# Reordering the first tile of a fused retention and gated-FFN kernel: wider zero products, keys and queries loaded ahead of values, one copy split over two engines

## The chip, the cores and the metric

The kernel runs on one core of one Trainium2 chip. A core has five instruction streams that run beside each other and meet only at semaphores: PE (matrix products; its weight loads are a track of their own, PEld), DVE and ACT (both copy and compute, and both read the accumulator banks that PE writes), POOL (GpSimd, which here also issues most of the transfers), and SP (which issues transfers only). The time of a run is the time on the device in microseconds, here from the one core that is used; a kernel's figure is the median over its runs. The profile is of one such run, and carries its own time.

## The reference, cut to what matters

Four batches of eight heads, 768 positions, 64 wide. First a recurrent retention with one decay per head, then a gated feed-forward layer over its output:

```python
gamma = 1.0 - 2.0 ** (-5.0 - np.arange(H))
for t in range(S):
    state = gamma * state + einsum('bhd,bhe->bhde', k[:, :, t], v[:, :, t])
    y[:, :, t] = scale * einsum('bhd,bhde->bhe', q[:, :, t], state)
x = y.transpose(0, 2, 1, 3).reshape(B * S, H * D)
gate = 1.0 / (1.0 + np.exp(-(x @ w_gate)))     # 512 -> 1536
out = (gate * (x @ w_val)) @ w_out              # 1536 -> 512
```

## The kernel before, in words

The 768 positions are cut in six tiles of 128 positions (`NT = 6`). A tile has the same 128 positions of all four batches, so the feed-forward layer sees 512 tokens per tile. Within a tile the retention is worked in two groups `i` of two batches `j` each; the texts below number the four as chunk 0 to 3, and write (i, j) for them. For a chunk, keys and queries are turned on PE (four products with the identity for each), copied out of the accumulator banks to `kqT`, multiplied to scores (eight half-height products), multiplied by a decay mask on DVE to bfloat16 (`st`, two instructions of 512 columns), and multiplied with the values to the outputs `y` (eight products). The scaled outputs of the four chunks fill the columns of `xT`, which the layer's products (`up_part`, L349: four products of 512 columns per gate or value column block) read. `down` (L376) is the layer's second product. PE's products write into eight accumulator banks that are handed out in turn (`pf`).

The program is in an order written out by hand: each engine runs its instructions in the order of the code. The first tile has code of its own, which the change is all about:

- L104 and L105 load keys and queries of chunk 0 in float32 through the queues of SP and ACT. L109 loads the other chunks, cast to bfloat16, through POOL, which takes them one after the other; L112 to L114 put the first six pieces of the gate and value weights behind them on the same queue. Piece 0 of the gate weights is what the very first `up_part` reads.
- L132 and L133 make `zero`, a constant of zeros. `keep_on` (L400) multiplies zeros with zeros into a bank that nobody reads. It is called eleven times before the layer's first product, with 3 to 40 products in a call, 104 in all.
- L137 to L151 make the constants on DVE and ACT, among them `decay`, and cast chunk 0. `later_constants` (L153), `later_exps` (L164), `last_exps` (L168, the table `taby` that tile 1 onward uses in `y_out`) and `last_constants` (L161) make the rest, in the midst of the first tile.
- `first_transpose` (L302), `first_scores` (L309) and `first_y` (L315) are the three steps of a chunk; their last argument is the engine that copies the result. L408 to L448 string them together. `first_scaled` (L326, POOL) and `first_state` make the state that the second tile needs; the sigmoid's table is loaded on ACT at L437.
- L449 begins the layer for tile 0.

Of the kernel before, what the change touches and what calls it, by code (L numbers as in the profile page):

```python
# [9 lines left out]
BF16 = mybir.dt.bfloat16  # L10
AX = mybir.ActivationFunctionType
ALU = mybir.AluOpType
# [3 lines left out]
def kernel(  # L16
# [12 lines left out]
    nc = tc.nc  # L29
# [4 lines left out]
    NT = S // C  # L34
    NP = H // 2
# [3 lines left out]
    scale = 1.0 / math.sqrt(D)  # L39
# [3 lines left out]
    const = ctx.enter_context(tc.tile_pool(name="const", bufs=1))  # L43
# [37 lines left out]
    def load_gate_val(s):  # L81
        load_w(wg, moe_w_gate, s)
        load_w(wv, moe_w_val, s)
# [7 lines left out]
    def first(dst, x, b, n, eng):  # L91
        eng.dma_start(out=dst, in_=x[b:b + n, :, 0:C, :].rearrange("b h s d -> s (b h) d"))  # L92
# [8 lines left out]
    def entry(t, j):  # L101
        return t[:, j * H:(j + 1) * H, :]
# [3 lines left out]
    nc.scalar.preload_act_table(AX.Exp)  # L106
    ahead = const.tile([128, C], F32, name="ahead")
    nc.gpsimd.iota(ahead, pattern=[[-1, C]], base=0, channel_multiplier=1, allow_small_or_imprecise_dtypes=True)
    for x, b in ((k, 1), (q, 1), (k, 2), (q, 2), (v, 0), (k, 3), (q, 3), (v, 1), (v, 2), (v, 3)):  # L109
        tiles = kn if x is k else qn if x is q else vs  # L110
        first(entry(tiles[b // 2], b % 2), x, b, 1, nc.gpsimd)
    load_gate_val(0)  # L112
# [6 lines left out]
    nlg = const.tile([128, 2, NP], F32, name="nlg")  # L119
    lgz = const.tile([128, 2, NP], F32, name="lgz")  # L120
    lsc = const.tile([128, 1], F32, name="lsc")
    tok = const.tile([128, NT], F32, name="tok")
    col = const.tile([128, C], F32, name="col")
    ident = const.tile([128, 128], BF16, name="ident")
    causal = const.tile([128, 128], F32, name="causal")
    decay = const.tile([128, 2, NP, C], F32, name="decay")
    maskk = const.tile([128, 2, NP, C], F32, name="maskk")
    tabs = const.tile([128, H, NT], F32, name="tabs")
    tabsk = const.tile([128, NT, 2, H], F32, name="tabsk")
    taby = const.tile([128, NP, C], F32, name="taby")  # L130
    tabz = const.tile([128, NT, 2, NP], F32, name="tabz")
    zero = const.tile([128, 128], BF16, name="zero")  # L132
    nc.vector.memset(zero, 0.0)  # L133
    nc.vector.memset(lsc, math.log(scale))
    for h in range(H):
# [11 lines left out]
    nc.vector.tensor_scalar(col, ahead, ahead[:, 0:1], -1.0, op0=ALU.subtract, op1=ALU.mult)  # L147
    for t in range(NT):
        nc.vector.tensor_scalar(tok[:, t:t + 1], ahead[:, 0:1], float(t * C), None, op0=ALU.add)
    nc.vector.tensor_copy(entry(kn[0], 0), kf)  # L150
    nc.scalar.copy(entry(qn[0], 0), qf)  # L151

    def later_constants():  # L153
        nc.vector.tensor_tensor(tabs.rearrange("s (p e) t -> s p e t", e=2),
                                tok.unsqueeze(1).unsqueeze(1).to_broadcast([128, NP, 2, NT]),
                                nlg.rearrange("s e p -> s p e").unsqueeze(3).to_broadcast([128, NP, 2, NT]), op=ALU.mult)

        for t in range(1, NT):
            nc.vector.tensor_scalar(tabz[:, t], lgz, float(t * C), None, op0=ALU.mult)

    def last_constants():  # L161
        nc.vector.tensor_scalar(causal, ahead, 0.0, None, op0=ALU.is_le)

    def later_exps():  # L164
        nc.scalar.activation(tabs, tabs, AX.Exp)
        nc.scalar.activation(tabz[:, 1:], tabz[:, 1:], AX.Exp)

    def last_exps():  # L168
        for p in range(NP):
            nc.scalar.activation(taby[:, p], col, AX.Exp, bias=lsc, scale=lgz[:, 0, p:p + 1])  # L170

    def later_tables():
        src = tabs.rearrange("s (p e) t -> s e t p", e=2)
# [12 lines left out]
    def bank(shape, dt=F32):  # L186
        return pf.tile(shape, dt, tag="ff", name="ff")

    def half(e):
        return slice(e * D, (e + 1) * D)  # L190

    def heads(t, j, p):
        return t[:, j * H + 2 * p:j * H + 2 * p + 2, :].rearrange("s h d -> s (h d)")

    def new_kqT(i):
        kqT[i] = at.tile([128, 2, 2, NP, C], BF16, tag="kqT", name="kqT", bufs=2)
# [19 lines left out]
    def scores(i, j):  # L216
        t = kqT[i]
        sc[i, j] = (bank([128, NP, C]), bank([128, NP, C]))
        for p in range(NP):
            for e in range(2):  # L220
                nc.tensor.matmul(sc[i, j][e][:, p, :], t[half(e), 0, j, p, :], t[half(e), 1, j, p, :],  # L221
                                 start=True, stop=True)
# [79 lines left out]
    def first_transpose(i, j, which, eng):  # L302
        x = (kn[i], qn[i])[which]
        tp = bank([128, NP, C], BF16)
        for p in range(NP):
            nc.tensor.transpose(tp[:, p, :], heads(x, j, p), ident)
        eng(kqT[i][:, which, j], tp)

    def first_scores(i, j):  # L309
        scores(i, j)  # L310
        for e, st in enumerate((stA, stB)):
            st[i, j] = at.tile([128, NP, C], BF16, tag=f"st{e}", name=f"st{e}", bufs=4)
            nc.vector.tensor_tensor(st[i, j], sc[i, j][e], decay[:, e], op=ALU.mult)  # L313

    def first_y(i, j, eng):  # L315
        if 0 not in xT:
            xT[0] = at.tile([128, NP, 512], BF16, tag="xT", name="xT")
        o = bank([128, NP, C])
        for p in range(NP):
            for e, st in enumerate((stA, stB)):  # L320
                nc.tensor.matmul(o[half(e), p, :], vs[i][:, j * H + 2 * p + e, :], st[i, j][:, p, :],  # L321
                                 start=(p == 0), stop=True, skip_group_check=True)
        c = (2 * i + j) * C
        eng(xT[0][:, :, c:c + C], o)
# [75 lines left out]
    def keep_on(n):  # L400
        u = bank([128, 512])
        for _ in range(n):
            nc.tensor.matmul(u[:, :128], zero, zero, start=True, stop=True)  # L403

    act, dve = nc.scalar.copy, nc.vector.tensor_copy
    new_kqT(0)  # L408
    new_kqT(1)
    keep_on(40)  # L410
    first_transpose(0, 0, 0, dve)
    first_transpose(0, 0, 1, act)
    later_constants()
    keep_on(3)
    first_transpose(0, 1, 0, act)
    first_scores(0, 0)
    first_transpose(0, 1, 1, act)
    keep_on(7)
    first_scores(0, 1)
    first_transpose(1, 0, 0, act)  # L420
    keep_on(3)
    first_transpose(1, 0, 1, act)
    keep_on(6)
    first_y(0, 0, act)
    later_exps()
    first_scores(1, 0)
    keep_on(4)
    first_transpose(1, 1, 0, act)
    last_exps()
    keep_on(5)  # L430
    first_transpose(1, 1, 1, dve)
    keep_on(6)
    first_y(0, 1, act)
    first_scores(1, 1)
    keep_on(6)
    first_y(1, 0, act)
    nc.scalar.preload_act_table(AX.Sigmoid)  # L437
    keep_on(12)
    first_y(1, 1, dve)
    last_constants()  # L440
    first_scaled(0, 0, kf)
    first_scaled(0, 1, entry(kn[0], 1))
# [2 lines left out]
    first_scaled(1, 1, entry(kn[1], 1))  # L445
    load_gate_val(4)
    load_gate_val(5)
    keep_on(12)  # L448
    for n1 in (0, 2, 4):  # L449
        gates = [up_part(0, wg, (n1 + i,)) for i in range(2)]  # L450
        for i in range(2):
# [111 lines left out]
```

## Time and profile before

| | |
|---|---|
| median of 4 runs | 229.94 us (229.79 to 230.27) |
| the profiled execution | 229.79 us |
| its span, first to last instruction | 228.0 us |
| PE busy | 220.1 us (97% of the span) |
| DVE, ACT, POOL busy | 110.0, 71.8, 104.0 us |
| first product of the layer (L349) starts | 16.92 us into the span |

The profile gives, per engine, what it did and what ended its idle times. Its parts used here are: the page's sums; the chain of waits, which starts at the last instruction and goes back, at each step, to whatever released it; the timeline, which lists the instructions of an engine in order of time with start and duration in us; and the transfers, with the time from the start of the issuing instruction to the landing of the data. A product on PE is recorded from its start to its end, some 0.2 us later, while the next ones have already started; so the distance between starts is what a product costs in a row of them. All times in the text are counted from the span's start.

### The profile page before, as it was taken

Reading aid. Unit: us, or ns where it says so; the run is one execution under the profiler, and the core shown is the slowest. Engines: PE = TensorE matmul, PEld = TensorE weight load, DVE = VectorE, ACT = ScalarE, POOL = GpSimd, SP = SyncE. Lnnn points to the kernel's source line nnn. Section 1 sums busy time; section 2 is a strip of 40 time slices with the busy share of each in tenths; the row PEclk is TensorE's granted clock in tenths of the full one; section 3 lists DMA queues with packets and bytes.
Section 4 is the critical chain, followed back from the end, with each engine's and each line's share of the span. In section 5 each row is a group of like instructions: output and inputs, shape, how many; then the busy total and the mean of one; then the engine's idle time right before and its main releaser. Section 6 shows DMA issues by size and latency. Waiting matters only on the chain.

```text
span 228.0 us, 4478 instructions
## 1 busy us (share of the span) xinstructions
PE 220.1 (97%) x1834; PEld 122.1 (54%) x1856; DVE 110.0 (48%) x198; ACT 71.8 (31%) x120; POOL 104.0 (46%) x125
## 2 busy tenths in 40 slices
PE   7789999999999999999999999999999999999994
PEld 7664444558888655445445445445444444444444
DVE  6663563064763776834905634914444812343301
ACT  4784233336323111332321433311433311433221
POOL 8999769999949969149930063000000000000000
PEclk9999999999999999999999999999999999999999
DMA  9999999999999999999992899012620012100022
GB/s 127 152 171 197 196 197 160 165 205 196 112 141 166 127 178 193 177 128 107 98 104 92 105 164 103 3 46 92 106 36 0 3 46 92 46 4 0 0 92 92
DMA packets 103636, 25.19 MB, mean 110 GB/s; under 512 B 92608, under 2 KB 100672, under 8 KB 103616
## 3 DMA queue, kind: packets, MB, share of 16 engines
q0 software_dynamic: 80896, 13.90, 82.8%
q1 hardware_dynamic: 21536, 10.69, 23.1%
q10 hardware_dynamic: 1184, 0.33, 0.6%
q8 instruction: 14, 0.23, 0.4%
q14 instruction: 6, 0.05, 0.1%
HBM read 28.31 MB, written 6.29 MB: 152 GB/s over the span
## 4 chain that ended last, share of the span: by engine, by line
PE 92%; POOL 3%; DMA 3%; issue 1%; DVE 0%; POOLq 0%
PE ff L349 55%; PE ff L376 26%; DMA vs<-in_v_dram 3%; PE ff L244 2%; PE ff L221 2%; PE ff L237 2%; POOL kn L92 1%; PE ff L389 1%; POOL qn L92 1%; PE ff L259 1%; PE ff L202 1%; POOL vs L92 1%; PE ff L403 1%; PE ff L321 0%; PE ff L335 0%
## 5 line engine op out<-in xcount | busy, mean ns | idle before, releaser
L360 DVE TENSOR_TENSOR hT<-gs,ff 128x512 bf16<-128x512 f32 x72 | 49.0, 686 | 62.8 <-PE ff L349 62.8
L349 PE MATMUL ff<-xT,wg 128*128 128x512 bf16 (+1 forms) x331 | 73.3, 348 | 0.5
L349 PE MATMUL ff<-xT,wv 128*128 128x512 bf16 (+1 forms) x331 | 72.8, 348 | 0.1
L359 ACT ACTIVATE gs<-ff 128x512 f32<-128x512 f32 x72 | 43.0, 597 | 83.9 <-PE ff L349 78.0
L376 PE MATMUL ff<-wo,hT 128*128 128x512 bf16 x264 | 61.0, 379 | 0.9 <-issue 0.5
L349 PEld LDWEIGHTS <-wv 128*128 128x128 bf16 x336 | 32.9, 98 | 29.4
L349 PEld LDWEIGHTS <-wg 128*128 128x128 bf16 x336 | 32.1, 98 | 28.5 <-issue 0.2
L376 PEld LDWEIGHTS <-hT 128*128 128x128 bf16 x276 | 26.2, 98 | 30.7
L380 ACT COPY ob<-ff 128x512 f32<-128x512 f32 x23 | 13.5, 585 | 58.6 <-PE ff L376 58.5
L227 DVE TENSOR_TENSOR st<-ff,maskk 128x512 bf16<-128x512 f32 x40 | 24.7, 680 | 6.4 <-PE ff L221 6.4
L252 DVE TENSOR_TENSOR xT<-ff,taby 128x512 bf16<-128x512 f32 x20 | 12.9, 686 | 30.8 <-PE ff L244 30.8
L213 POOL TENSOR_TENSOR ks<-kn,tabsk 128x1024 bf16<-128x1024 bf16 x8 | 16.3, 2034 | 0.0
L67 POOL DMA_DIRECT2D qn<-in_q_dram x20 | 15.4, 797 | 1.1 <-DMA wv<-in_moe_w_val_dram 0.6
L67 POOL DMA_DIRECT2D kn<-in_k_dram x20 | 15.1, 771 | 0.8 <-DMA wg<-in_moe_w_gate_dram 0.6
L507 POOL COPY held<-kqX 128x1 bf16<-128x1 bf16 x6 | 1.2, 207 | 29.5 <-DMA kqX<-qn 29.5
L57 POOL DMA_DIRECT2D vs<-in_v_dram x10 | 12.2, 1218 | 0.0
L403 PE MATMUL ff<-zero 128*128 128x128 bf16 x104 | 9.2, 248 | 1.0 <-DVE zero L133 1.0
L63 POOL DMA_DIRECT2D kn<-in_k_dram x10 | 9.4, 941 | 0.9 <-issue 0.9
L63 POOL DMA_DIRECT2D qn<-in_q_dram x10 | 9.2, 921 | 0.6 <-DMA wv<-in_moe_w_val_dram 0.6
L403 PEld LDWEIGHTS <-zero 128*128 128x128 bf16 x104 | 7.7, 114 | 1.4 <-DVE zero L133 1.0
L272 DVE TENSOR_TENSOR zb<-za,tabz 128x512 bf16<-128x512 f32 x10 | 6.8, 687 | 0.2
L313 DVE TENSOR_TENSOR st<-ff,decay 128x512 bf16<-128x512 f32 x8 | 5.2, 686 | 2.6 <-PE ff L221 1.4
(69 smaller groups left out, 118.8 us busy)
## 6 DMA issues: line engine op xcount, KB each, us to landing
out_dram<-ob SPq DMA_DIRECT2D x23, 256.0 KB, 2.0
vs<-in_v_dram POOLq DMA_DIRECT2D x10, 256.0 KB, 6.5
kn<-in_k_dram POOLq DMA_DIRECT2D x13, 128.0 KB, 5.1
qn<-in_q_dram POOLq DMA_DIRECT2D x13, 128.0 KB, 5.4
wg<-in_moe_w_gate_dram POOLq DMA_DIRECT2D x6, 256.0 KB, 7.5
wv<-in_moe_w_val_dram POOLq DMA_DIRECT2D x6, 256.0 KB, 8.0
wo<-in_moe_w_out_dram POOLq DMA_DIRECT2D x4, 384.0 KB, 8.3
kn<-in_k_dram POOLq DMA_DIRECT2D x20, 64.0 KB, 5.4
```

What stands on the lines that cost most here:

```text
L57: nc.gpsimd.dma_start(out=vs[i], in_=v[2 * h:2 * h + 2, :, t * C:(t + 1) * C, :].rearrange("b h s d -> s (b h) d"))
L63: nc.gpsimd.dma_start(out=tiles[i][:, 0:H], in_=src[0])
L67: nc.gpsimd.dma_start(out=dst[:, e], in_=pairs[:, 1 - e])
L213: nc.gpsimd.tensor_tensor(ks[i], kn[i], tabsk[:, i // 2].rearrange("s j h -> s (j h)").unsqueeze(2) .to_broadcast([C, 2 * H, D]), op=ALU.mult)
L227: nc.vector.tensor_tensor(st[i, j], sc[i, j][e], maskk[:, e ^ j], op=ALU.mult)
L252: nc.vector.tensor_tensor(xT[t][:, :, c:c + C], y[i, j], taby, op=ALU.mult)
L349: nc.tensor.matmul(u[:, i * n:(i + 1) * n], w[:, kk, n1 * 128:(n1 + 1) * 128], xT[t][:, kk, lo:hi], start=(kk == 0), stop=(kk == KT - 1))
L359: nc.scalar.activation(g, ps[0], AX.Sigmoid)
L360: nc.vector.tensor_tensor(hT[t][:, n1s[0]:n1s[-1] + 1, lo:hi], g.rearrange("p (i n) -> p i n", n=n), ps[1].rearrange("p (i n) -> p i n", n ...
L376: nc.tensor.matmul(o, hT[t][:, n1, b * C:(b + 1) * C], wo[:, n1, :], start=(n1 == 0), stop=(n1 == NFF - 1))
L380: nc.scalar.copy(ob, o)
L403: nc.tensor.matmul(u[:, :128], zero, zero, start=True, stop=True)
```

## The change

In the setup, keys and queries of chunk 3 are loaded ahead of values of chunk 0; the zeros are 512 columns wide, and a zero product takes its 128 weights from their first 128 columns and streams all 512. The table `tabs` is set up, and `taby` computed, ahead of the casts of chunk 0. In the first tile the calls of `keep_on` go from 104 products of 128 columns to 26 of 512 columns (19 at the start, then six calls of one or two); the scores of a chunk come ahead of the outputs `y` of earlier ones; chunk (1, 1)'s output is copied by `split`, of which DVE takes the first two of the four 128-row blocks of the model's width (`kk` in `up_part`) and ACT the other two; and the sigmoid's table is loaded behind that copy instead of ahead of the last `y`.

```diff
-    for x, b in ((k, 1), (q, 1), (k, 2), (q, 2), (v, 0), (k, 3), (q, 3), (v, 1), (v, 2), (v, 3)):
+    for x, b in ((k, 1), (q, 1), (k, 2), (q, 2), (k, 3), (q, 3), (v, 0), (v, 1), (v, 2), (v, 3)):
...
-    zero = const.tile([128, 128], BF16, name="zero")
+    zero = const.tile([128, 512], BF16, name="zero")
...
+    nc.vector.tensor_tensor(tabs.rearrange("s (p e) t -> s p e t", e=2),
+                            tok.unsqueeze(1).unsqueeze(1).to_broadcast([128, NP, 2, NT]),
+                            nlg.rearrange("s e p -> s p e").unsqueeze(3).to_broadcast([128, NP, 2, NT]), op=ALU.mult)
+    for p in range(NP):
+        nc.scalar.activation(taby[:, p], col, AX.Exp, bias=lsc, scale=lgz[:, 0, p:p + 1])
     nc.vector.tensor_copy(entry(kn[0], 0), kf)
     nc.scalar.copy(entry(qn[0], 0), qf)
...
-            nc.tensor.matmul(u[:, :128], zero, zero, start=True, stop=True)
+            nc.tensor.matmul(u, zero[:, :128], zero, start=True, stop=True)
...
+    def split(dst, src):
+        dve(dst[:, 0:2], src[:, 0:2])
+        act(dst[:, 2:4], src[:, 2:4])
...
-    keep_on(40)
+    keep_on(19)
     first_transpose(0, 0, 0, dve)
     first_transpose(0, 0, 1, act)
     later_constants()
-    keep_on(3)
     first_transpose(0, 1, 0, act)
     first_scores(0, 0)
     first_transpose(0, 1, 1, act)
-    keep_on(7)
+    first_transpose(1, 0, 0, act)
+    keep_on(1)
     first_scores(0, 1)
-    first_transpose(1, 0, 0, act)
-    keep_on(3)
     first_transpose(1, 0, 1, act)
-    keep_on(6)
+    keep_on(2)
+    first_scores(1, 0)
+    first_transpose(1, 1, 0, act)
+    later_exps()
+    first_transpose(1, 1, 1, dve)
+    keep_on(1)
     first_y(0, 0, act)
-    later_exps()
-    first_scores(1, 0)
-    keep_on(4)
-    first_transpose(1, 1, 0, act)
-    last_exps()
-    keep_on(5)
-    first_transpose(1, 1, 1, dve)
-    keep_on(6)
+    first_scores(1, 1)
     first_y(0, 1, act)
-    first_scores(1, 1)
-    keep_on(6)
+    keep_on(1)
     first_y(1, 0, act)
+    keep_on(1)
+    first_y(1, 1, split)
     nc.scalar.preload_act_table(AX.Sigmoid)
-    keep_on(12)
-    first_y(1, 1, dve)
     last_constants()
...
-    keep_on(12)
+    keep_on(1)
     for n1 in (0, 2, 4):
```

## The prediction

> **What bounds the kernel now.** The page first: PE is busy nearly all of the span, so the end moves only if PE gets less to do, or starts its long stretch sooner.
>
> ```profile
> span 228.0 us, 4478 instructions
> PE 220.1 (97%) x1834; PEld 122.1 (54%) x1856; DVE 110.0 (48%) x198; ACT 71.8 (31%) x120; POOL 104.0 (46%) x125
> ```
>
> The list of waits, asked for PE from 17 us to the end, names 0.5 us in three idle gaps, none of them for a transfer. So from the layer's first product (L349) PE runs through, and its start sets the end. The chain of waits shows what sets that start.
>
> ```profile
> 7.62 0.80 POOL vs L92
> 8.42 6.04 DMA vs<-in_v_dram
> 14.46 0.04 issue
> 14.51 0.41 PE ff L321 x8
> 14.92 0.78 PE ff L403 x12
> 15.70 0.34 PE ff L321 x8
> 16.04 0.78 PE ff L403 x12
> 16.82 0.10 issue
> 16.92 0.38 PE ff L349
> ```
>
> To be seen: values of chunk 2 land at 14.46, eight products of `y`, then twelve zero products stand ahead of the last `y` (15.63), then twelve more. The values of chunk 3 were issued at 9.29 and took 5.6 us, so they were there at 14.9: about 0.7 us of the chain is zero products that nothing needed. DVE's timeline gives the work that ran beside, and POOL's the transfer that comes next:
>
> ```profile
> 12.44 0.42 DVE L307 COPY kqT<-ff 128x512 bf16<-128x512 bf16 x1
> 13.66 1.29 DVE L313 TENSOR_TENSOR st<-ff,decay 128x512 bf16<-128x512 f32 x2 [0.80 <-PE ff L221]
> 16.08 0.69 DVE L324 CAST xT<-ff 128x512 bf16<-128x512 f32 x1 [1.14 <-PE ff L321]
> ...
> 9.29 0.95 POOL L92 DMA_DIRECT2D vs<-in_v_dram  x1
> 10.15 0.84 POOL L79 DMA_DIRECT2D wg<-in_moe_w_gate_dram  x1
> ...
> wg<-in_moe_w_gate_dram POOLq DMA_DIRECT2D x1, 256.0 KB, 6.0
> ```
>
> The masks of the last chunk end at 14.95. The first gate weights, issued at 10.15, land 6.0 later (16.20 by the record): with `xT` copied at 16.77 they had 0.6 us to spare, and become the next limit.
>
> The last reading is of the clock. L403 asked for in a window at the start, and in one after 4.67:
>
> ```profile
> L403 PE MATMUL ff<-zero x31: 288/314/315, 1.0 to 4.2; 128*128 128x128 bf16 x31
> ...
> L403 PE MATMUL ff<-zero x6: 219/220/220, 4.5 to 4.8; 128*128 128x128 bf16 x6
> ```
>
> Zero products start 107 ns apart up to 4.38 us and 56 ns apart from there; the record of the granted clock also begins at 4.37, 3.38 us after the first product. Before that PE runs at half speed.
>
> **The change part by part.** *Opening zeros.* A memset of 64 words took 112 ns, of one word 59; on that line 256 words take 0.27, so the zeros start at 1.16 instead of 0.99. 512 columns cost 216 ns each at full clock (the spacing of L349: eight in 1.73 us) and four times 107, 427 ns, before. If full clock again comes 3.38 us after the start (4.54), eight are slow (to 4.57) and eleven fast (2.37): the zeros end at 6.95. Bounds: all fast, 5.26; all slow, 9.27. I take 6.95, as the wait for the clock is a measured one. Before, the last of them started at 4.77 and the first transposes at 5.41, so this part makes the chain 1.5 us late; the rest has to be followed.
>
> *Constants.* `tabs` (0.20) fits in DVE's idle 0.75 ahead of L150. The four exps of `taby` (1.65) run on ACT from 4.35 (behind `col`, 4.17 plus the memset's 0.16) to 6.0, the cast of q (0.62) to 6.62; its transposes are not reached until 7.17. Nothing, hidden by the zeros; without them 0.33 late. In return ACT has 1.65 less among the copies.
>
> *The rows of the first tile, in the new order.* From the timeline: a group of four transposes is copied from 0.43 after its start (5.41 to 5.84), 0.42 on DVE, 0.58 on ACT; scores start 0.06 after the copy (7.36 to 7.42), their masks 0.49 later and take 1.29; PE goes on 0.33 after scores start. So: transposes of k0 at 6.95 and q0 at 7.17, copied at 8.19; scores 8.25, masks 8.74 to 10.03. q1 turned behind those scores at 8.58, copied 9.01 to 9.60; scores 9.66, masks 10.15 to 11.44. q2 (lands 9.27) turned at 9.99, copied to 11.00; scores 11.06, masks to 12.84. q3 waits on DVE behind these masks: copied to 13.28 by DVE; scores 13.34, masks 13.83 to 15.12. Before, they ended at 14.95: the chain of copies and masks, not transfers, now sets this pace.
>
> *Loads.* Four issues of equal length trade places on POOL (0.87 each); k3 and q3 land a place or two earlier (10.17, 11.07, in the slots of v0 and k3), v0 at 11.96 instead of 10.17. What is behind, v1 (12.84) to the weights, keeps its slot. Turning k3 and q3 comes at 11.4 or later, so their earlier landing buys 0.5 us at most. `y` of chunk 0 waits for v0 until 12.0; PE then waits for q3's copy until 13.34, so this costs nothing. If the scores did not wait there it would cost up to 1.8, the move itself.
>
> *The end of the chain.* `y` of chunk 2 at 14.51 as before; one zero product; `y` of chunk 3 needs v3 (14.9) and the second mask (15.12): 15.17 for its later half, against 15.63. Its copy starts 0.45 later, 15.62. In the built program ACT's half waits for DVE's half, and the first two products of the layer need only DVE's. A half on DVE lies between 0.28 (128 columns, L138) and 0.69 (512); by the line through them 0.42: done at 16.04, and with the 0.15 from 16.77 to 16.92, PE could start at 16.19. ACT's half (0.25 for L165 to 0.58 for L324; 0.45 taken) ends at 16.5, before the third product at 16.25 + 0.43: hidden. But the gate weights are there at 16.20, and a weight load started 0.04 after its data (14.46 to 14.51): 16.25. So the layer starts at 16.25 instead of 16.92, 0.67 earlier, the chain 0.06 from being the limit itself.
>
> *Sigmoid's table.* Behind ACT's half: 16.5 to 17.8. The first sigmoid came 1.06 after the layer's start (17.98), so would be due at 17.31: 0.5 late. ACT was idle 1.99 before the third, and its bank is not wanted for seven more groups: nothing, 0.5 at most.
>
> *Behind it.* The next weights landed at 17.53, 18.92, 20.23, 21.55, 23.38; PE needs them at 17.98, 19.70, 21.43, 23.62, 25.36: 0.45 to spare at the least. Keys and queries for L202 landed by 38.20 and are wanted at 39.4. Everything else that PE waits for follows PE. The gain should reach the end whole.
>
> *Sum.* The profiled execution took 229.79, 1.8 beside its span; less 0.67, 229.12. The median of the runs is 0.15 above that execution: 229.94 - 0.67 = 229.27, say 229.3.
>
> *A rule against it.* The Trainium skill (TensorE: Matmul & The Clock Gate, "What's actually happening") says that the clock is released after a busy window of 3.4 us on a grid that does not start with the kernel; this trace's 3.38 would then be the luckiest case, and with the grid at its worst 16 of the zeros are slow, ending near 8.6 and putting the sum near 230.9. One trace cannot tell the two apart.
>
> **The rivals.** *Clock late (slower).* Place: the opening zeros. Each microsecond of later clock makes them 0.5 later (427 against 216), and the chain from there has 0.06 to spare, so it passes on. Point: zeros ending after 6.95 + 0.06 + 0.67 = 7.68 lose time. All slow (9.27) is 2.26 later than free, less 0.67: 231.5; halfway 230.4. For: zeros were 40 x 107 before, done long before they were needed, so runs before could not show such a delay. Against: 3.38 in the one trace.
>
> *Clock lost (slower).* Between 7 and 16 us zeros fall from 64 x 56 = 3.6 us to 6 x 216 = 1.3. A fall to half speed into the layer for as long as the release took, 3.4 us, costs 1.7: 231.0. Against: from 4.37 to 7.78 PE had 25 transposes and zeros and eight scores, some 1.6 us of 3.41, and kept its clock; the new order's thinnest such stretch, from about 11.8, has 1.5.
>
> *Transfer takes it back (same).* The values of chunk 2 took 6.0 where their four predecessors took 5.2 to 5.3. Such a stretch at the first gate weights puts them at 16.9, and the layer where it was: 229.9. The same follows if the copies and masks take 0.6 more in all. Half of either: 229.6. For: both have under 0.1 to spare. Against: bytes and order ahead of the weights are the same.
>
> **How the numbers follow.** Forecast 0.50, own range 229.0 to 229.5; transfer or chain takes most of it 0.24, 229.5 to 230.3; clock late 0.15, 230.4 to 231.5; clock lost 0.07, 230.5 to 231.5; better than forecast, 0.04 (weights 0.4 sooner, at 15.8, as v3's 5.6 would have it, and a shorter chain: 228.8). Two tenths of a percent is 0.46 us, about what can be told from no change: faster 0.52, same 0.25, slower 0.23. The range, 228.9 to 230.7, leaves out the upper part of both clock cases and the best one.
>
> **What would show it.** Zeros ending near 6.95, with eight 427 ns apart; scores starting near 8.3, 9.7, 11.1, 13.3; last masks ending near 15.1; L349 first at 16.25 behind the gate weights, ACT's half done before its third product; no idle PE after. It is wrong if the zeros run past 7.7, if products of 512 columns come 427 apart after 5 us, or if PE waits on a transfer after its start.

## The result, and the profile after

The changed kernel's median is 229.42 us (228.46 to 230.19, 52 runs) against 229.98 us (229.40 to 231.93, 76 runs) for the kernel before: a ratio of 0.9965, 95% interval 0.9955 to 0.9974. It is 0.56 us faster, a quarter of a percent, inside the range and on the side that was forecast. The page of the profiled execution (229.68 us) begins:

```profile
span 227.9 us, 4323 instructions
PE 219.9 (96%) x1755; PEld 117.9 (52%) x1778; DVE 110.1 (48%) x198; ACT 72.1 (32%) x121; POOL 103.8 (46%) x125
```

That one run is hardly faster than the profiled run of before (229.79). Why not is in its chain of waits up to 20 us (start, duration, what):

```profile
0.86 0.28 DVE zero L133
1.15 0.05 issue
1.19 6.86 PE ff L400 x19
8.06 0.46 PE ff L303 x8
8.52 0.02 issue
8.54 0.59 ACT kqT L304
...
12.41 1.28 DVE st L310 x2
13.69 0.34 DVE kqT L304
...
15.74 0.49 PE ff L318 x8
16.23 0.02 issue
16.25 0.44 DVE xT L407
16.69 0.14 issue
16.83 3.18 PE ff L346 x14
```

To be seen: no transfer is left in the chain. It begins with the opening zeros, which run 6.86 us, and goes on through copies, scores and masks to the layer's first product at 16.83. The zeros asked for by their line, in a window up to 6.2 us (duration min/median/max in ns, first and last start):

```profile
L400 PE MATMUL ff<-zero x12: 609/634/634, 1.2 to 5.9; 128*128 128x512 bf16 x12
```

Twelve at half clock instead of the eight that were reckoned with: the record of the granted clock begins at 6.47, 5.28 us after the first product, where the run of before had 3.38 (the record itself is in the trace; the products' spacing, 427 ns up to there and 216 behind, agrees with it). The split copy on ACT's timeline (start, duration, engine, line, operation, idle before and who ended it):

```profile
15.53 0.59 ACT L321 CAST xT<-ff 128x512 bf16<-128x512 f32 x1
16.71 0.37 ACT L408 CAST xT<-ff 128x256 bf16<-128x256 f32 x1 [0.60 <-DVE xT L407]
17.10 1.28 ACT L436 ACT_TABLE_LOAD   x1
18.40 1.08 ACT L356 ACTIVATE gs<-ff 128x512 f32<-128x512 f32 x2
```

ACT's half waits for DVE's, ends at 17.09 ahead of the third product, and the table load then holds the first sigmoid until 18.40, without any wait on PE.

The times of these eight profiled runs tie to one number, the start of the layer. In this table "release" is where the record of the full clock begins, "turned" the first transposes, "layer" the first product of L346 (L349 before):

| run | first zero | release | turned | layer | run's time less layer |
|---|---|---|---|---|---|
| before | 0.99 | 4.37 | 5.41 | 16.92 | 212.87 |
| changed | 1.19 | 6.47 | 7.89 | 16.83 | 212.85 |
| e13 (changed, one cast later) | 1.19 | 4.14 | 6.75 | 15.68 | 212.91 |
| e9 (changed, old load order) | 1.19 | 4.96 | 7.15 | 16.08 | 213.48 |
| e5 (changed, 23 zeros) | 1.19 | 6.06 | 8.55 | 17.48 | 212.88 |
| e4 (changed, whole copy) | 1.19 | 6.72 | 8.01 | 17.21 | 212.85 |
| e7 (narrow opening, late zeros) | 1.19 | 6.92 | 5.43 | 16.25 | 212.93 |
| e6 (before, scores first) | 0.99 | 5.33 | 5.31 | 16.02 | 212.87 |

Read downwards: what comes behind the layer's start takes 212.9 (e9 is met below, with e1, e8 and e11, which end later too; e3, e10 and e12 fit, at 212.84 to 212.86). Read across, wherever 19 or 23 wide zeros open and the split copy closes, the layer starts 8.93 or 8.94 us after the first transposes. So in these four traces, all with the wide opening, the layer's start is set by when the clock is released, and by nothing else.

### The profile page after: what moved, and what is told of

Same layout as the page of the kernel before. It is cut to its first block, busy times and chain, and to the rows that moved or that the text cites. A ratio compares the mean times of both kernels' runs of the same rounds, so it can differ in the third digit from the quotient of the medians.

```text
span 227.9 us, 4323 instructions
## 1 busy us (share of the span) xinstructions
PE 219.9 (96%) x1755; PEld 117.9 (52%) x1778; DVE 110.1 (48%) x198; ACT 72.1 (32%) x121; POOL 103.8 (46%) x125
## 4 chain that ended last, share of the span: by engine, by line
PE 96%; DVE 1%; issue 1%; ACT 1%
PE ff L346 55%; PE ff L373 26%; PE ff L400 3%; PE ff L218 3%; PE ff L241 2%; PE ff L234 2%; PE ff L386 1%; PE ff L256 1%; ACT kqT L304 1%; PE ff L199 1%; DVE st L310 1%; PE ff L318 1%; PE ff L303 1%; PE ff L332 0%; DVE xT L407 0%
## 5 line engine op out<-in xcount | busy, mean ns | idle before, releaser
L346 PE MATMUL ff<-xT,wg 128*128 128x512 bf16 (+1 forms) x331 | 73.2, 348 | 0.7 <-DVE xT L407 0.3
L346 PE MATMUL ff<-xT,wv 128*128 128x512 bf16 (+1 forms) x332 | 72.8, 348 | 0.1
L346 PEld LDWEIGHTS <-wv 128*128 128x128 bf16 x336 | 32.9, 98 | 29.4
L346 PEld LDWEIGHTS <-wg 128*128 128x128 bf16 x336 | 32.1, 98 | 28.9 <-DMA wg<-in_moe_w_gate_dram 0.6
L210 POOL TENSOR_TENSOR ks<-kn,tabsk 128x1024 bf16<-128x1024 bf16 x8 | 15.8, 1981 | 0.0
L67 POOL DMA_DIRECT2D kn<-in_k_dram x20 | 15.1, 770 | 0.9 <-DMA wg<-in_moe_w_gate_dram 0.6
L400 PE MATMUL ff<-zero 128*128 128x512 bf16 x24 | 8.8, 510 | 1.2 <-DVE zero L133 1.2
L269 DVE TENSOR_TENSOR zb<-za,tabz 128x512 bf16<-128x512 f32 x10 | 7.3, 734 | 0.2
L241 PE MATMUL ff<-st,vs 128*64 128x128 bf16 x160 | 6.4, 222 | 0.0
L400 PEld LDWEIGHTS <-zero 128*128 128x128 bf16 x26 | 3.1, 123 | 5.4 <-issue 3.5
```

Source lines behind the costliest of these rows:

```text
L67: nc.gpsimd.dma_start(out=dst[:, e], in_=pairs[:, 1 - e])
L210: nc.gpsimd.tensor_tensor(ks[i], kn[i], tabsk[:, i // 2].rearrange("s j h -> s (j h)").unsqueeze(2) .to_broadcast([C, 2 * H, D]), op=ALU.mult)
L346: nc.tensor.matmul(u[:, i * n:(i + 1) * n], w[:, kk, n1 * 128:(n1 + 1) * 128], xT[t][:, kk, lo:hi], start=(kk == 0), stop=(kk == KT - 1))
L400: nc.tensor.matmul(u, zero[:, :128], zero, start=True, stop=True)
```

## The experiments

Each was made from the changed kernel unless the kernel before is named; "runs" are its timed runs, and the ratio is to the kernel before, run on the same chip.

**e1: the old opening.**

```diff
-    keep_on(19)
+    keep_narrow(40)     # 40 products, 128 columns each
```

> The changed kernel with the opening of the kernel before: 40 zero products of 128 columns in place of 19 of 512; all else as changed. Theory A (the chain of the first tile starts when the opening zeros end, and their length hangs on when the clock is released): the zeros end near 5.2 us whatever the clock does, the transposes start near 5.4, the last masks end near 14 at the latest, and the layer's first product starts right behind its gate weights, near 16.3 instead of 16.83; median 0.3 to 0.6 us under the changed kernel, and the spread of its runs narrower than the 1.7 us of the changed kernel. Theory B (the opening is not on the path; the gain comes from the zeros taken out ahead of the last y): the median stays where the changed kernel is, 229.4, with the same spread. Theory C (wide zeros are needed to release the clock): runs of 231 to 232, more of them than the kernel before has.

Median 229.70 (12 runs), ratio 0.9983 (0.9956 to 1.0010). The runs fall in two heaps: seven from 228.91 to 229.72, five from 230.64 to 231.35. The profiled one is the slowest, and shows why, in four stretches of 3.41 us (length, PE busy and instructions, granted clock; the last two columns, on transfers, are not used here):

```profile
10.69:14.10 3.41, 2.68 (x43) 1.00 2.57 160
14.10:17.51 3.41, 1.43 (x13) 1.00 1.44 191
17.52:20.93 3.41, 3.41 (x10) 0.50 1.45 196
20.94:24.35 3.41, 3.41 (x18) 1.00 1.45 196
```

To be seen: PE was busy 1.43 of 3.41 us, as it stood from 14 us on for the last values (landed 15.75), and for the whole next stretch the clock was halved; the layer had just started (16.82). Its ten products there came 427 ns apart. Against 212.9, 1.7 us more were needed behind the layer's start. So a short opening does free the chain (first transposes at 5.31, masks done by 14.1), as theory A has it, and the seven lower runs have a median of 229.17; but A's median, 0.3 to 0.6 under 229.42, is missed. Runs of over 230.6 come too, much as theory C has it, but not for its reason: the clock came early (3.87) and was lost again. The mean granted clock of every timed run is on record and says the same of the whole upper heap: 0.991 to 0.993 in those five runs, 1.000 in the other seven.

**e3: the kernel before, without the twelve zeros ahead of the last y.**

```diff
-    keep_on(12)
     first_y(1, 1, dve)
```

> The kernel before without the twelve zero products between the y of chunk 2 and the y of chunk 3; all else as before. Theory A and B: the last y starts at 14.95 at the earliest instead of 15.63, its copy ends near 16.1, and the layer starts near 16.25, behind the gate weights: 0.5 to 0.7 us faster than the kernel before, as much as the whole change. If the gate weights land later than in the one trace of before, less: 0.2 to 0.4. Theory C (these zeros keep the clock): slower by 1 us or more.

Median 229.93 (12 runs), ratio 0.9987 (0.9967 to 1.0007): no gain that can be told, against 0.5 to 0.7 expected (the interval does not quite exclude 0.7). Its PE timeline:

```profile
13.63 0.41 PE L321 MATMUL ff<-st,vs 128*64 128x128 bf16 x8 [1.23 <-DMA vs<-in_v_dram]
13.97 0.40 PE L221 MATMUL ff<-kqT 64*128 64x128 bf16 x8
```

and DVE's:

```profile
14.41 1.29 DVE L313 TENSOR_TENSOR st<-ff,decay 128x512 bf16<-128x512 f32 x2 [1.88 <-PE ff L221]
```

The values of chunk 1 landed at 13.58 here (12.84 in the profiled run of before). PE, in order, waits for them at that chunk's y with the last scores behind it; the masks end at 15.70, and the layer starts at 17.01 with the zeros gone.

**e6: the same, and the scores of chunk 3 ahead of the y of chunk 1.**

```diff
-    first_y(0, 1, act)
     first_scores(1, 1)
+    first_y(0, 1, act)
```

> The kernel before without the twelve zero products ahead of the last y, as in the run before it, and now also with the scores of chunk 3 ahead of the y of chunk 1. Theory A (in that run PE stood at the y of chunk 1 until its values landed, and the scores and masks of chunk 3 were stuck behind it): the last masks end near 14.5 whatever the values do, the layer starts near 16.2, behind its gate weights or behind the copy: 0.4 to 0.8 us under the kernel before. Rival (removing zeros or moving scores is no use, since the transfers set the start): within 0.2 of the kernel before.

Median 229.05 (228.89 to 229.67, five runs), ratio 0.9964 (0.9952 to 0.9976). The same two timelines, PE's

```profile
12.71 0.40 PE L221 MATMUL ff<-kqT 64*128 64x128 bf16 x8 [0.18 <-DVE kqT L307]
13.63 0.41 PE L321 MATMUL ff<-st,vs 128*64 128x128 bf16 x8 [0.52 <-DMA vs<-in_v_dram]
```

and DVE's:

```profile
13.13 1.29 DVE L313 TENSOR_TENSOR st<-ff,decay 128x512 bf16<-128x512 f32 x2 [0.47 <-PE ff L221]
```

The values land as late as in e3 (13.59), but the masks are under way by then, and the layer starts at 16.02 behind its gate weights (15.98). Two lines moved or taken out of the old order give what the whole change gives, as far as five runs tell.

**e4: the last copy whole.**

```diff
-    first_y(1, 1, split)
+    first_y(1, 1, dve)
```

> The changed kernel with the last x copied whole by DVE (0.69 us) in place of two halves. Theory A: in runs whose chain ends last, the layer starts 0.26 later (0.69 against the 0.43 of the half); in runs where the gate weights come last, nothing: median 0.1 to 0.25 us above the changed kernel. Rival: the weights always come last, no difference within 0.05.

Median 229.29 (12 runs), ratio 0.9949 (0.9922 to 0.9976): as the changed kernel, so its times don't settle it. The trace does: DVE's copy starts 0.47 behind the last y, as before, but takes

```profile
16.37 0.69 DVE L321 CAST xT<-ff 128x512 bf16<-128x512 f32 x1 [0.47 <-PE ff L318]
```

and the layer starts 9.20 after the first transposes, not 8.94: the 0.26 of theory A, in a run that the chain bounds. Against a spread of more than a microsecond, 12 runs can't show it.

**e5: four more opening zeros.**

```diff
-    keep_on(19)
+    keep_on(23)
```

> The changed kernel with 23 wide zero products at the start in place of 19. Theory A: four more at full clock, 0.86 us, all of it on the chain where the chain ends last, and 0.86 less the spare time where the weights come last: median 0.5 to 0.9 us above the changed kernel. Theory B: no difference, as the opening is hidden behind the loads.

Median 230.10 (229.43 to 230.69, 12 runs), ratio 0.9993 (0.9972 to 1.0014): 0.68 above the changed kernel, where theory A said 0.5 to 0.9 and B nothing. The opening is on the path.

**e9: the loads in the old order.**

```diff
-    ... (k, 3), (q, 3), (v, 0), (v, 1) ...
+    ... (v, 0), (k, 3), (q, 3), (v, 1) ...
```

> The changed kernel with the loads in the order of the kernel before: v0 ahead of k3 and q3. Theory A (q3's transposes are reached at 12.5, after it has landed in either order): no difference, within 0.15 of the changed kernel. Rival (the loads' order is what brings the gain): 0.4 to 0.6 above it.

Median 229.28 (seven runs), ratio 0.9966 (0.9953 to 0.9979): no difference, as theory A has it. Its profiled run shows something else. It started the layer at 16.08 and should have ended 0.6 sooner than it did. Near 112 us, on DVE's timeline,

```profile
112.39 2.37 DVE L269 TENSOR_TENSOR zb<-za,tabz 128x512 bf16<-128x512 f32 x1
114.68 0.68 DVE L357 TENSOR_TENSOR hT<-gs,ff 128x512 bf16<-128x512 f32 x1
```

on POOL's,

```profile
112.22 1.98 POOL L210 TENSOR_TENSOR ks<-kn,tabsk 128x1024 bf16<-128x1024 bf16 x1
```

and on PE's:

```profile
115.41 1.25 PE L373 MATMUL ff<-wo,hT 128*128 128x512 bf16 x5 [0.32 <-DVE hT L357]
```

This is the operation of `casts` (L269), which scales a pair's state and writes it in bfloat16. By itself it takes 0.69 (mean of the ten in the profiled run of the kernel before). Here it takes 2.37, and ends half a microsecond after POOL's scaling of keys; PE then waits for the product behind it. In the profiled run of the changed kernel the same two met for the last half microsecond (the cast took 1.15), without a wait on PE. PE's work moves with the layer's start; POOL waits for transfers (5.9 us for one of them, some 15 us before), and in the 14 traces this scaling of it began anywhere from 110.0 (e13) to 113.8 us (before). So whether the two meet here hangs on POOL's time at least as much as on an early start: e11, whose layer began at 16.72, hardly ahead of the changed kernel's 16.83, met it worst. The same cast was stretched at other places too (2.25 at 52 us and 2.18 at 80 in e3, 2.23 at 86 in e7) without loss at the end, so it is only here that PE was seen to pay.

**e7 and e8: a short opening, and zeros where PE waits anyway.** e7 has 40 narrow products at the start, e8 13 wide ones; both have

```diff
-    keep_on(1)
+    keep_on(3)
     first_y(1, 0, act)
-    keep_on(1)
+    keep_on(2)
     first_y(1, 1, split)
...
     load_gate_val(5)
-    keep_on(1)
+    keep_on(3)
```

> The changed kernel with the opening of the kernel before (40 zeros of 128 columns), and more wide zeros where PE waits for the last values and the last copy: 3, 2 and 3 in place of 1, 1 and 1. Theory A (with the short opening alone, the runs at 230.6 to 231.4 are those in which PE was too idle for one window of 3.4 us and lost the clock at the layer's start, and the others show what the short opening brings): the runs over 230.5 go (0 or 1 of 12, from 5 of 12), and the median is 228.8 to 229.3. Rival (the slow runs come from a late first release, as the opening is too short): they stay, 4 to 6 of 12.

> The changed kernel with 13 wide zeros at the start in place of 19, and the same late zeros as in the run before. Theory A: the opening ends 1.3 (released at once) to 2.6 (all slow) earlier than in the changed kernel, 6.8 at the latest, which is long enough for the release; the chain then ends at 15.7 at the latest, and the layer waits for its weights: no run over 230.5, median 228.7 to 229.2. If the release needs the 19, a tail of 231 as with the narrow opening.

e7: median 229.31 (229.16 to 229.83, 11 runs), ratio 0.9972 (0.9958 to 0.9985). The upper heap of e1 is gone, so it hung on the idle stretch and not on a late first release (which in e7's profiled run came at 6.92, against 4.37 in that of before and 3.87 in the profiled run of e1). Its chain now ends the way that was forecast for the changed kernel:

```profile
10.15 6.06 DMA wg<-in_moe_w_gate_dram
16.21 0.05 issue
16.25 1.90 PE ff L346 x8
```

e8: median 229.23 (228.74 to 229.59, five runs), ratio 0.9968 (0.9956 to 0.9980); none of the five above 229.6, so 19 do not look needed for the release. Its layer started at 16.46, and the chain to there runs through the late zeros: the last y starts 1.98 behind that of chunk 1 (13.45 to 15.43), against 1.33 in e13, so these zeros were not free. 0.28 were lost later where the cast and the scaling met (2.15 for the cast).

**e10 and e11: the first weights in halves**, on top of e7, the gate piece alone and the value piece too.

```diff
-    load_gate_val(0)
+    load_cols(wg, moe_w_gate, 0, 128)
+    load_cols(wg, moe_w_gate, 128, 256)
+    load_w(wv, moe_w_val, 0)
```

> The run with the narrow opening and late zeros (e7), its first gate piece loaded as two pieces of 128 columns. Theory A (with a short opening the layer's start waits for the first gate piece, 256 columns, of which the first four products need only half): the first half lands 0.5 to 0.7 earlier, near 15.4, the layer starts 15.5 to 15.8 instead of 16.25, and the second half and the value piece are there in time or cost 0.2 at most: 0.3 to 0.6 under e7, 228.7 to 229.0. Rival (the next pieces, or the work behind, set the pace, as the later wait of some runs suggests): no more than 0.15 under e7.

> As e10, and the first value piece in two as well. Theory A: the value half lands before it is needed at 1.73 after the start; equal to e10 or up to 0.2 faster. Rival: the additional issue on POOL (0.75) pushes the pieces behind back, and PE waits for the second gate piece: slower than e10 by 0.2 to 0.6.

Both miss: 229.53 (12 runs), 0.9975 (0.9960 to 0.9991), and 229.65 (12 runs), 0.9974 (0.9955 to 0.9993); no better than e7. In e11 the first half landed at 16.67, later than the whole piece in e7 (16.21). In e10 another transfer was late, as its chain shows:

```profile
9.28 6.63 DMA vs<-in_v_dram
15.92 0.04 issue
15.96 0.41 PE ff L323 x8
```

The same load of the last values landed at 14.3 in e7, 14.2 in the changed kernel, 15.75 in e1, 15.37 in e12. A late transfer turns up somewhere between 13 and 17 us in most runs; what makes it late was not found. e11's run also lost 0.7 where cast and scaling meet (2.48 for the cast, PE waiting at 115).

**e12 and e13: that cast four groups later**, on top of e7 and of the changed kernel.

```diff
-    ... (10, casts, 7), (10, xbar, 8),
+    ... (14, casts, 7), (10, xbar, 8),
```

> The run with the narrow opening and late zeros (e7), with the cast of state 7 moved from behind group 10 to behind group 14 of tile 2. Theory D (where the layer starts early, this cast on DVE meets POOL's scaling of keys at 112 us, ends only when that ends, and PE waits up to 0.6 us for the product behind it): the wait near 115 us is gone, the run's time is its layer's start plus 212.9 in the profiled run, and the median falls by 0.1 to 0.3, to 229.0 to 229.2. Rival (the meeting is rare or moves to the next place): no change of the median, within 0.1.

> The changed kernel with the cast of state 7 moved in the same way. Theory D: in its earlier starting runs 0.3 to 0.6 are won, in its later ones nothing: median 229.1 to 229.4 against 229.42, the slowest runs near 230.2 as before, as these hang on the clock's release. Rival: 229.4, no difference.

229.31 (228.95 to 229.56, 12 runs), 0.9968 (0.9954 to 0.9982), and 229.37 (228.59 to 230.00, 12 runs), 0.9967 (0.9947 to 0.9987). Neither trace has a wait near 115 us, and both end 212.9 after the layer's start, e13 from the earliest start of all (15.68); but the medians didn't move, so what the meeting costs over many runs is not shown. e13's chain has the opening near its best case (release 2.95 us after the first zero):

```profile
1.19 5.71 PE ff L400 x19
6.91 0.46 PE ff L303 x8
...
15.11 0.43 DVE xT L407
15.54 0.14 issue
15.68 2.53 PE ff L346 x11
```

5.71 us of zeros against 6.86, and the layer starts 1.15 earlier.

By their medians e6 to e9, e12 and e13 can't be told from the changed kernel: they lie at 0.9964 to 0.9972 with intervals that overlap its own. The spread may differ: 0.7 and 0.6 us between the fastest and slowest of e7 (11 runs) and e12 (12), 1.4 in e13 (12) and 1.7 in the changed kernel (52). But e10 and e11, also with the short opening, have 1.1 and 1.2 (12 each), so a smaller spread is not shown for the short opening as such.

## Why the prediction held, step by step

*Direction and size.* Forecast 0.67 faster, measured 0.56. The size is right for a reason that the forecast had as its rival, and the agreement is partly luck: in the changed kernel's own trace the first transposes come 0.94 later than reckoned (7.89 against 6.95), and 0.30 of that is made good by a chain that is shorter than reckoned.

*The step that failed* is in the opening zeros: "If full clock again comes 3.38 us after the start ... I take 6.95, as the wait for the clock is a measured one". It was measured once, and it isn't one number. In the 13 traces that recorded it the release came 2.65 to 5.98 us after the first zero. With each microsecond of it the zeros end 0.49 later (427 against 216 ns each), so by 1.19 + 19 x 0.216 = 5.29 and 0.49 for each microsecond the first transposes come between 6.6 and 8.25 (the same sum gives the four traces with 19 zeros to 0.02), and with 8.94 and 212.9 the runs between 228.4 and 230.1. Measured: 228.46 to 230.19. The two ends of the release were traced in other openings (e12, e8), and the untraced runs have no release on record, so that their whole spread is the clock's follows from this agreement alone. "Clock late", which had 0.15, is thus no case beside the forecast but its other half, and its shape was right: half a microsecond for each, passed on down the chain. Its price for all zeros slow (231.5) never fell due, as in every trace with 19 or 23 zeros the clock came before they were over. The "rule against it" that the prediction named, a grid that does not start with the kernel, is what the traces show (last section); its worst case of 16 slow zeros and 230.9 was not met, as the latest release, 5.98, makes 14.

*The chain behind the zeros.* Reckoned from the first transposes, scores were to start at 1.30, 2.71, 4.11 and 6.39, and did at 1.29, 2.69, 4.09 and 6.18; the copies were to let the layer start at 9.24, and did at 8.94. The 0.2 in the last scores is q3's copy, which DVE reached sooner. The rows of before gave each step to a few hundredths.

*"But the gate weights are there at 16.20 ... So the layer starts at 16.25."* Not in the changed kernel: in its own trace, and in those of e4, e5, e9 and e13, the copy came last, up to 2 us behind the weights (landed 15.13 to 16.27). In e6, e7 and e11, where the opening is short, the weights did come last, and the layer started at 16.02, 16.25 and 16.72.

*"About 0.7 us of the chain is zero products that nothing needed."* True of the one trace, not of the kernel: taking them out brought nothing that can be told (e3), since in both other traces made from the kernel before (e3, e6) values of chunk 1 land 0.7 later and hold PE, in e3 ahead of the last scores. By the traces the scores moved forward are what counts (e6), a part that was followed through the chain but given no term of its own; the intervals of e3 and e6 (0.9967 to 1.0007, 0.9952 to 0.9976) still overlap.

*Loads, constants, split, sigmoid's table.* Loads nothing, as said (e9). The exps of `taby` and the cast of q behind them were done by 6.37, long ahead of their transposes. DVE's half copy took 0.42 against 0.42, ACT's 0.37 against 0.45, ahead of the third product. The first sigmoid was held by the table and PE did not notice. The memset took 0.28 against 0.27, and the zeros started at 1.19 against 1.16.

*"The gain should reach the end whole."* In most traces it does: 212.8 to 212.9. In three (e8, e9, e11) 0.3 to 0.7 us went where the cast on DVE meets POOL, a place that the prediction did not look for, as nothing waits there in the trace of before: there the cast ended at 113.78, just as POOL's scaling began.

*Clock lost.* Not seen in the changed kernel: none of its 52 runs is above 230.19 or has a mean granted clock under 0.998, and the thinnest full stretch of its trace had PE busy 2.41 of 3.41. (The prediction's 1.6 and 1.5 add up the spacings of starts; by the recorded busy time its stretch of before, 4.37 to 7.78, had 2.17.) The rival was real for its neighbour e1, at the price that was reckoned, 1.7.

It was real for the kernel before as well, which the prediction did not see. Runs of before were made again beside the experiments, with their mean granted clock on record: 12 of 99 took 231.48 to 231.92 us at a clock of 0.990 to 0.993, the other 87 at most 230.52 at 0.998 or more. One stretch of 3.41 us at half speed in 230 us makes 0.993. So before lost the clock in about one run in eight, and the changed kernel, with less filler between 7 and 16 us, in none of 52.

*Transfer takes it back.* The last values land anywhere from 14.2 to 15.9 and the first weights from 15.1 to 16.7. In the traces with the long opening the values came by 14.6 and the weights by 16.3, both ahead of their use, so what late ones would cost there is not shown.

*Left open:* nine of the 76 runs of before lie at 231.4 to 231.9. They have no clock on record and none was profiled; the time is that of the 12 runs above, but in which stretch before loses its clock, and why in some runs only, was not traced.

## What to carry to other kernels

Where a stretch of filler work opens a kernel to bring the clock up, its length in time is that of the slow products in it, and it varies from run to run; take short products and let the real work start as soon as it can, or reckon the spread as part of the path. Filler is free only where the engine waits for a transfer or a copy anyway (in e8 it was not), and is needed there if the wait is long (e1). A mean clock of 0.993 over a run, small as the difference looks, marks a run that lost 1.7 us. When the work of two engines is timed by different things, look for places where they may meet, also far behind the place that was changed.

## What the runs showed of the hardware

*The clock moves on a grid of its own.* From release to the last drop, 225.28 us in the trace of before and 221.87 in that of the changed kernel, are 66 and 65 times 3.4133 us; in e1 the stretches are 4, 1 and 61 times that. PE's busy time over a cell of the grid fits what was decided at its end in every trace. The cell at whose end the clock was released had PE busy 3.37 us of 3.41 or more, but for 2.65 in e12, 2.68 in e1, 2.95 in e13 and 3.07 in e7; cells with 2.57 (e8) and 2.32 (e7) at the start did not release it. Once up, it stayed through cells with as little as 2.01 (e1) and 2.02 (e12), and went after the one with 1.43. So the grid that the Trainium skill describes (TensorE: Matmul & The Clock Gate, "What's actually happening") is what the runs show. The page puts the scatter at half a microsecond to either side, and has the clock go after an idle window; here it was 1.7 to either side, and a window two fifths busy was enough to lose it.

*DVE is held by POOL.* The cast with two operands in SBUF took 0.69 us alone; begun 0.38, 0.17 and 0.06 us into POOL's scaling it took 2.15, 2.37 and 2.48 (e8, e9, e11), ending each time about 0.55 after POOL did. DVE's multiplications into `hT`, with one operand in an accumulator bank, kept their 0.69 beside the same POOL operation (e9, 104.09 and 105.82). The other way round POOL waits: its scaling, 1.98 us else, took 2.44 when it began 0.01 us into a cast that kept its 0.69 (e4, at 79.97), and 2.35 when 0.10 into one (before, at 52.12). The Trainium skill (SBUF — State Buffer, "Summary: rules for kernel authors") says that of two operations like the cast and this scaling the second fully waits for the first, and these numbers agree.
